# Block transposes for the second batch element's dense pairs, and up products between them

## The chip, the cores and the metric

The kernel runs on one core of a Trainium2 chip. The metric is the device time of one execution in microseconds (us); 1039.21 us is the median of three runs of the kernel before.

## What is computed

```python
q_assign = np.argmax(np.einsum('bhsd,hcd->bhsc', q_n, c_n), axis=-1)   # q, k, centroids normalised
k_assign = np.argmax(np.einsum('bhsd,hcd->bhsc', k_n, c_n), axis=-1)
mask = q_assign[:, :, :, None] == k_assign[:, :, None, :]
scores = scale * np.matmul(q, k.transpose(0, 1, 3, 2))
scores = np.where(mask, scores, -1000000000.0)
attn = np.exp(scores - scores.max(-1, keepdims=True))
attn = attn / (np.sum(attn, axis=-1, keepdims=True) + 1e-09)
x = np.matmul(attn, v)           # then (B,H,S,D) -> (B*S, H*D)
out = (x @ w_a) * (x @ w_b) @ w_out
```

The shapes are 4 batch elements, 8 heads, 768 tokens, head width 64, 16 clusters; model width 512, inner width 1536; all in fp32. The weights arrive as 64-bit numbers.

## The kernel before

Two heads make a pair, so there are 16 pairs, four to a batch element. Pairs 0 to 7 (batch elements 0 and 1) are computed densely: every score is formed and the mask is added as a product of one-hot cluster codes. The other eight are "sorted pairs" n = 1 to 8: their tokens are written to DRAM in the order of clusters, read back, and only scores within a cluster are formed. The feed-forward part follows for each batch element; its work is cut into pieces that a planner puts between other steps. All instructions are in an order that the program writes out while it is built, with a model clock (`now`, `clocks`, `spend`, `at`); on the chip each engine's queue runs in that order and waits on semaphores.

**Dense pairs** (`score`, `weigh`, `add_up`, `denominators`, `normalize`). A pair has two halves of 384 queries and six tiles of 128 keys, so 12 units; a group is two units, a pair six groups (l = 0 to 5), all of them 48. In each group TensorE forms the mask and the scores into two `ps_s` tiles (L497), ScalarE takes the exponential (L507), TensorE multiplies by v (L537), and the exponentials of a half are added up (L526), by GpSimd in pair 0 and by VectorE in the others, as two instructions of 128x384. Every third group the sums go through a product with ones (`denominators`, L555) and are inverted (L575 to L589).

**Preparing the next pair** (`prep_steps`). While pair p runs, pair p+1 is prepared step by step at l = 0 to 5: q and k are transposed on TensorE (`prep_transpose`, L361, copied out at L369), multiplied by the centroids (`prep_sim`, L377, L382), transposed back (`prep_across`, L388), turned into a one-hot on VectorE (`prep_assign`, L421 to L425, from `todo`), transposed as bf16 (`prep_onehot`, L434) and copied by ScalarE (L439, L442). `apart` gives these steps a tile: of `ps_m` as long as no feed-forward product has run, of `ps_s` afterwards.

**Sorted pairs** (`sorted_pair`). Each has a chain of steps with gaps and gates: `load_rows` (L1136), `across` (L1147, L1152), `similarities` (L1158), `assign` (L1178 to L1190), `prefix` (L1205, L1207), `index` (`find`, L1230 to L1257, and `after`), 24 indirect writes by GpSimd (`put`, L1308), `reload` (L1335, L1339), turns on VectorE (L1347), `scores` (L1376), `values` (L1401, L1410), `keep`, 12 indirect reads (`get`, L1440) and `x_across` (L1455). The first EARLY = 3 are sorted while the dense pairs run, in borrowed room; the rest after the dense pairs, in the tile `whole`, which takes their room (`late_room`). DRAM buffers go in a ring of three, cleared by `clear` (L1109, L1111).

**Weights** (`round_one`, `round_w`). Each of 36 parts is loaded (L278) and cut to fp32 by four VectorE instructions (L289 to L299), two of ScalarE (L303, L304) and an addition on GpSimd (L307).

**Feed-forward.** For batch element 0 the up products (`ffn_block`, pieces of 8 products over two column halves, L615) go block by block; the later batch elements and all down products use a scheme with seven products instead of eight (`ffn_ups`, `ffn_downs`). `in_turn` rotates three `ps_m` tiles. `PER_GROUP = 0` keeps all pieces out of the dense groups:

```python
    PER_GROUP = 0
    credit = 0
```

Each line of DMA on the sync engine (SP) is issued in order, and a waiting one holds the rest.

Of the kernel before, what the change touches and what calls it, by code (L numbers as in the profile page):

```python
# [34 lines left out]
P = 128  # L35
# [122 lines left out]
def short_path(nc, tc, ctx, c, cn, centroids_in, casts, n_far, q, k, v,  # L158
# [14 lines left out]
    SPACE, EARLY = 2.0, 3  # L173
# [4 lines left out]
    V, Vs, Vc, Vh, Vm, Vl = (Clocked(nc.vector, "V", us, *state)  # L178
                             for us in (0.56, 0.19, 0.29, 0.44, 0.7, 0.83))
    S_, Ss, Sl = (Clocked(nc.scalar, "S", us, *state) for us in (0.5, 0.3, 0.85))  # L180
    G_, Gi = (Clocked(nc.gpsimd, "G", us, *state) for us in (1.3, SPACE))
# [38 lines left out]

    def load(p):
        if p >= ND:
            return
        b, hp = divmod(p, HP)
        if p == 1:
# [26 lines left out]
    def load_v(p):  # L252
# [4 lines left out]
        vs[p] = t  # L257
        nc.sync.dma_start(
# [64 lines left out]

    idle = ps_o.tile([P, 512], FP32, name="O")
# [46 lines left out]
    def prep_sim(p):  # L371
# [4 lines left out]
        for kq in range(4):  # L376
# [3 lines left out]
                             start=True, stop=True)  # L380
        t = simp.tile([P, HB], FP32, name="sim")
# [78 lines left out]

    def prep_steps(p):
# [3 lines left out]
        def both(*fs):  # L465
            return lambda: [f() for f in fs]

# [50 lines left out]
    def add_up(u):  # L518
# [5 lines left out]
        acc = accs[p, hf]  # L524
        for a in range(2):
            (G_ if p == 0 else V).tensor_tensor(  # L526
                out=acc[:, a, :],
                in0=probs[u - 1][:, a, :] if j == 1 else acc[:, a, :],
                in1=probs[u][:, a, :], op=ALU.add)
# [89 lines left out]
    def store(b, j, half, y):  # L619
        rows = out[b * S:(b + 1) * S, :].rearrange(  # L620
            "(p j) (half n) -> p j half n", j=NJ, half=2)
# [21 lines left out]
    def ffn_block(b, blk):  # L643
# [14 lines left out]
        def piece_a(f):  # L658
# [3 lines left out]
            if f == 0:  # L662
# [3 lines left out]
                box["h"] = hp_.tile([P, NF, HB], FP32, name="h")  # L666
# [359 lines left out]
    kvd = [dram.tile([2 * ROWS + 32, 2 * D], FP32, name=f"kvd{n}") for n in range(3)]  # L1026
    qd = [dram.tile([2 * ROWS + 32, D], FP32, name=f"qd{n}") for n in range(3)]
# [14 lines left out]
    wanted = {}  # L1042
# [30 lines left out]
    def early_room():  # L1073
        t = hp_.tile([P, NF * HB], FP32, name="h")
        rooms([t[:, 0:ROW], t[:, ROW:2 * ROW]], extra[:, 2 * S:4 * S],
# [31 lines left out]
    def clear(n):  # L1107
        for m in range(n, NSORT, HP - 1):
            nc.sync.dma_start(out=od[m][2 * ROWS:], in_=zrow[0:32, 0:D])  # L1109
        for t, w in ((kvd[n % 3], 2 * D), (qd[n % 3], D)):  # L1110
# [11 lines left out]
    def sorted_pair(n, start):  # L1122
# [5 lines left out]
        parity, ring = n % 2, n % 3  # L1128
# [306 lines left out]
        def get(j, a):  # L1435
            if j == 0 and a == 0:
                if b not in xTs:
                    xTs[b] = xtp.tile([P, NCH, S], FP32, name="xT")
                M["xs"] = xTs[b][:, HP - 1].rearrange("p (j e) -> p j e", j=NJ)
# [40 lines left out]
        def may_load():  # L1480
            if n <= EARLY:
# [4 lines left out]
        chain += [plan(FREE, 7 if i == 0 else 0.3, lambda i=i: across(i),  # L1486
                       lambda: "P" not in busy and was("sims", n - 1), "T")
                  for i in range(3)]
# [6 lines left out]
                     lambda: was("clear", n, 8) if n < HP else was("reload", n - 3, 3))  # L1495
# [8 lines left out]
                     lambda: x_room() and (hp == 0 or was("x", n - 1)))  # L1504
# [518 lines left out]
```

## Time and profile before

| | |
|---|---|
| runs | 1038.17, 1039.21, 1040.02 us |
| profiled execution | 1039.23 us, its span 1037.2 us |
| TensorE (PE) busy | 985.5 us, 95% |
| VectorE (DVE) busy | 618.6 us, 60% |
| ScalarE (ACT) busy | 292.8 us, 28% |
| GpSimd (POOL) busy | 365.8 us, 35% |
| mean granted TensorE clock | 0.978 |

Busy times are shares of the span, from the first to the last instruction. "PEld" is TensorE's weight load, which overlaps its products. A row of the stretches gives the start and end, the length, and each engine's busy time in it with the number of instructions; then the granted clock, the DMA engines' share and GB/s. A row of a group gives line, engine, operation, tiles and shape, count, busy time, mean ns of one, and the idle time ahead of it with what ended it. A row of waits gives who waited for whom: us in total, times, longest.

### The profile page before, as it was taken

The page shows a single profiled execution, that of the slowest core. Times are in us where ns is not written, and L with a number is a line of the kernel's source. Part 1 is how long each engine was busy: PE and PEld are TensorE (multiplying, and loading weights), DVE is VectorE, ACT ScalarE, POOL GpSimd, SP SyncE. Part 2 cuts the span into 40 slices and gives each one's busy share as a digit, 9 for nine tenths or more (in the row PEclk, how much of TensorE's full clock was granted, in tenths as well). Part 3 has the DMA queues.
Part 4 walks back from the last instruction along what each step waited for, and adds up shares of the span by engine and source line. Part 5 has one row for each costly group of instructions (what it writes and reads, how often), then busy time and mean ns, then how long its engine had stood idle before and what let it go on. Part 6 is the DMA issues. An engine that isn't in the chain of part 4 may idle for free.

```text
span 1037.2 us, 20702 instructions
## 1 busy us (share of the span) xinstructions
PE 985.5 (95%) x8074; PEld 513.7 (50%) x8074; DVE 618.6 (60%) x1290; ACT 292.8 (28%) x609; POOL 365.8 (35%) x359
## 2 busy tenths in 40 slices
PE   8979998999799999989999899999999997999997
PEld 5434444443355545556444546654444763444564
DVE  5898897998476764846744775353335533334442
ACT  5636775775223322001122220021221101121100
POOL 3635563554105454433544453354441021000000
PEclk9989998999899999989999999999999998999999
DMA  9963642334978557392338533542327222222301
GB/s 235 248 155 103 169 144 63 94 102 110 184 151 168 152 120 121 122 179 59 88 76 145 119 83 131 106 113 79 82 75 155 87 52 60 59 62 61 118 29 32
DMA packets 242873, 116.51 MB, mean 112 GB/s; under 512 B 175696, under 2 KB 228944, under 8 KB 242768
## 3 DMA queue, kind: packets, MB, share of 16 engines
q1 hardware_dynamic: 233136, 102.08, 41.4%
q0 software_dynamic: 9216, 12.60, 4.8%
q8 instruction: 66, 1.08, 0.5%
q10 hardware_dynamic: 416, 0.43, 0.1%
q14 instruction: 39, 0.32, 0.1%
HBM read 79.46 MB, written 35.59 MB: 111 GB/s over the span
## 4 chain that ended last, share of the span: by engine, by line
PE 80%; DVE 12%; DMA 2%; SPq 2%; issue 2%; ACT 2%; POOL 0%; DVEq 0%; ACTq 0%
PE m L615 62%; PE s L497 4%; PE O L537 3%; DVE acc L526 3%; PE s L1376 2%; PE s L1401 2%; PE m L555 2%; PE s L1410 1%; SPq L1136 1%; PE m L361 1%; PE O L1147 1%; PE s L1455 1%; DVE rest L299 1%; DMA whole<-kvd 1%; SPq L1335 1%
## 5 line engine op out<-in xcount | busy, mean ns | idle before, releaser
L1440 POOL DMA_INDIRECT xT<-od,idx x96 | 94.3, 983 | 162.8 <-PE m L615 157.8
L615 PE MATMUL m<-xT,wb_sb 128*64 128x384 f32 x672 | 119.4, 494 | 1.3 <-DVE h L791 1.3
L615 PE MATMUL m<-xT,wa_sb 128*64 128x384 f32 x672 | 120.2, 495 | 0.0
L1308 POOL DMA_INDIRECT qd<-whole,idx x60 | 61.3, 1021 | 92.9 <-PE m L615 71.3
L791 DVE TENSOR_TENSOR ha<-ha,m 128x384 f32<-128x384 f32 x72 | 39.7, 551 | 89.6 <-PE m L615 68.6
L615 PE MATMUL m<-wo_sb,h 128*64 128x256 f32 x768 | 89.0, 387 | 0.0
L791 DVE TENSOR_TENSOR h<-h,m 128x384 f32<-128x384 f32 x72 | 39.8, 553 | 81.7 <-PE m L615 62.5
L788 ACT COPY h<-m 128x384 f32<-128x384 f32 x72 | 34.4, 478 | 187.4 <-PE m L615 184.1
L1308 POOL DMA_INDIRECT kvd<-whole,idx x60 | 61.3, 1022 | 66.7 <-PE m L615 57.3
L615 PE MATMUL m<-raw 128*64 128x384 f32 x432 | 79.0, 487 | 1.0 <-DVE raw L753 1.0
L507 ACT ACTIVATE pt<-s 128x768 f32<-128x768 f32 x96 | 72.7, 807 | 25.1 <-PE s L497 18.8
L615 PEld LDWEIGHTS m<-xT,wb_sb 128*64 128x64 f32 x672 | 48.2, 139 | 60.3 <-issue 53.8
L615 PEld LDWEIGHTS m<-xT,wa_sb 128*64 128x64 f32 x672 | 48.2, 139 | 58.5 <-issue 53.9
L537 PE MATMUL O<-pt,v 128*64 128x384 f32 x384 | 72.3, 498 | 0.0
L497 PE MATMUL s<-qkT 64*128 64x384 f32 x384 | 71.8, 494 | 0.0
L615 PEld LDWEIGHTS m<-wo_sb,h 128*64 128x64 f32 x768 | 55.5, 140 | 30.2 <-issue 3.7
L615 PE MATMUL m<-xT,h 128*64 128x256 f32 x576 | 65.0, 380 | 0.8 <-DVE h L903 0.8
L526 DVE TENSOR_TENSOR acc<-acc,pt 128x384 f32<-128x384 f32 x84 | 58.6, 754 | 2.4 <-ACT pt L507 2.4
L1308 POOL DMA_INDIRECT kvd<-h,idx x36 | 38.1, 1058 | 61.2 <-PE s L497 36.1
L615 PE MATMUL m<-xT,size 128*64 128x384 f32 x288 | 53.3, 491 | 3.0 <-DVE ha L791 3.0
L615 PEld LDWEIGHTS m<-xT,h 128*64 128x64 f32 x576 | 40.9, 137 | 21.8 <-issue 1.4
L615 PEld LDWEIGHTS m<-raw 128*64 128x64 f32 x432 | 30.6, 137 | 39.5 <-issue 36.8
(258 smaller groups left out, 1526.7 us busy)
## 6 DMA issues: line engine op xcount, KB each, us to landing
whole<-kvd SPq DMA_DIRECT2D x64, 160.0 KB
raw<-in_moe_w_a_dram SPq DMA_DIRECT2D x12, 512.0 KB
raw<-in_moe_w_b_dram SPq DMA_DIRECT2D x12, 512.0 KB
raw<-in_moe_w_out_dram SPq DMA_DIRECT2D x12, 512.0 KB
raw<-up_sums SPq DMA_DIRECT2D x96, 64.0 KB
whole<-qd SPq DMA_DIRECT2D x32, 160.0 KB
od<-whole SPq DMA_DIRECT2D x32, 160.0 KB
kvd<-xT SPq DMA_DIRECT2D x3, 1280.0 KB
```

The source lines that it names most:

```text
L497: ins = nc.tensor.matmul(out=s[:, a, 0:HB], lhsT=Ts[p][r, S + j * P:S + (j + 1) * P], rhs=Ts[p][r, hf * HB:(hf + 1) * HB], start=start, st ...
L507: Sl.activation(out=pt, in_=s[:, :, 0:HB], func=AF.Exp, scale=SCALE)
L526: (G_ if p == 0 else V).tensor_tensor(out=acc[:, a, :], in0=probs[u - 1][:, a, :] if j == 1 else acc[:, a, :], in1=probs[u][:, a, :], op=A ...
L537: ins = nc.tensor.matmul(out=O_of[0][a * D:(a + 1) * D, 0:HB], lhsT=vs[p][:, a, j, :], rhs=probs[u][:, a, :], start=(j == 0), stop=(j == N ...
L555: nc.tensor.matmul(out=ps[a * D:(a + 1) * D, 0:HB], lhsT=ones, rhs=t[:, a, :], start=(n == 0), stop=(n == len(terms) - 1))
L615: ins = nc.tensor.matmul(out=ps[half], lhsT=lhsT[:, half], rhs=rhs, **kw)
L788: S_.copy(out=box[name], in_=box["X"][:, 0:HB])
L791: V.tensor_tensor(out=box[name], in0=box[name], in1=box[bank][:, 0:HB], op=ALU.add)
L1308: ins = Gi.indirect_dma_start(out=dst[:, :], out_offset=bass.IndirectOffsetOnAxis(ap=M["idx"][:, w, j, a:a + 1], axis=0), in_=src, in_offs ...
L1376: nc.tensor.matmul(out=tiles[s // 2][r0:r0 + m, s % 2, c0:c0 + m], lhsT=M["skT"][r, h, 32 * x:32 * x + m], rhs=M["sqT"][r, h, 32 * x:32 * ...
L1401: nc.tensor.matmul(out=ps[:, s, 65 * i:65 * i + 65], lhsT=pt[:, P * i:P * i + P], rhs=vt[:, i, :], start=True, stop=True)
L1440: paced(Gi.indirect_dma_start(out=M["xs"][:, j, a * D:(a + 1) * D], out_offset=None, in_=od[n][:, :], in_offset=bass.IndirectOffsetOnAxis( ...
```

## The change

It does these things together:

- Pairs 4 to 7 (`by_blocks`) load q and k in 32-column blocks, so that VectorE's 32x32 block transposes give the transposed q and k, the transposed similarities, and the one-hot across; eight DMAs then place the one-hot's rows in `ohT`. TensorE's transposes and ScalarE's copies for these pairs go away. Their tokens keep the natural order, so v is loaded and the output is stored in it.
- The additions of pairs 1 to 7 become one instruction of 128x768.
- Feed-forward pieces are put into the dense groups: half a piece's cost is credited per group. Denominators then stand behind the next piece.
- Four sorted pairs are early instead of three (EARLY), and the DRAM ring has four buffers; their starts move to 76, 104, 150 and 150 of the model clock. The two `h` buffers are the borrowed room itself.
- Planner constants, gaps and gates change: the gap before a late pair's `across` is 12 instead of 7, before `x_across` 8 instead of 5; gathers may go ahead of the previous pairs' `x_across`.

```diff
-    SPACE, EARLY = 2.0, 3
+    SPACE, EARLY, RING = 2.0, 4, 4
...
+        if by_blocks(p):
+            t = qkp.tile([P, 2, S // 32, 32], FP32, name="qk")
+            for w, src in enumerate((q, k)):
+                for n in range(4):
+                    a, d = divmod(n, 2)
+                    nc.sync.dma_start(
+                        out=t[32 * n:32 * n + 32, w],
+                        in_=src[b, 2 * hp + a, :, 32 * d:32 * d + 32].rearrange(
+                            "(j t) d -> t j d", t=32))
...
+    def prep_by_blocks(p):
...
+        oh = oh_all[:, 0:3].rearrange("p n (g c) -> p (n g) c", c=NC)
+        ohT = oh_all[:, 3:6].rearrange("p n e -> p (n e)")
...
+        def across(w):
+            Vl.transpose(out=qkTs[p][:, w * S:(w + 1) * S],
+                        in_=qks[p][:, w].rearrange("p j d -> p (j d)"))
+
+        def sims_across():
+            V.transpose(out=sim.rearrange("p g c -> p (g c)"),
+                        in_=sims[p][:, 0:HB])
+
+        def one_hot():
+            V.tensor_tensor(out=oh[KT], in0=sim[KT], in1=top(first)[KT],
+                                    op=ALU.subtract)
+            V.tensor_tensor(out=oh[QT], in0=sim[QT], in1=top(first)[QT],
+                            op=ALU.is_equal)
+
+        def one_hot_across():
+            V.transpose(out=ohT, in_=oh.rearrange("p g c -> p (g c)"))
+            for a in range(2):
+                for kq in range(4):
+                    r = 32 * kq + a * NC
+                    nc.sync.dma_start(
+                        out=ohTs[p][a * D:a * D + NC, kq * HB:(kq + 1) * HB],
+                        in_=ohT[r:r + NC, :])
...
+        if p == HP:
+            return [[lambda: across(0), lambda: across(1)], [sims_across],
+                    assign[:2], assign[2:], [one_hot, one_hot_across], []]
+        return [[lambda: across(0), lambda: across(1)], [sims_across],
+                assign, [one_hot], [one_hot_across], []]
...
+        if p > 0:
+            Vd.tensor_tensor(out=acc, in0=probs[u - 1] if j == 1 else acc,
+                             in1=probs[u], op=ALU.add)
+            return
...
-                box["h"] = hp_.tile([P, NF, HB], FP32, name="h")
+                box["h"] = early[blk].rearrange("p (f t) -> p f t", f=NF)
...
-        chain += [plan(FREE, 7 if i == 0 else 0.3, lambda i=i: across(i),
+        chain += [plan(FREE, (12 if n > EARLY else 7) if i == 0 else 0.3, lambda i=i: across(i),
...
-                     lambda: x_room() and (hp == 0 or was("x", n - 1)))
+                     lambda: x_room() and (hp < 2 or was("x", n - (4 - hp))))
         chain += [plan(FREE, 0, lambda: mark("get", n)),
-                  plan(FREE, 5, x_across, kind="T")]
+                  plan(FREE, 8, x_across,
+                       lambda: hp == 0 or was("x", n - 1), "T")]
...
-                late = {"V": 2.2 if is_late else 7.0, "G": 1.8}.get(kind)
+                late = {"V": 2.2 if is_late else 4.0, "G": 2.6}.get(kind)
...
-            ffn.extend(counted(0, blocks[0][0][0:8]))
+            ffn.extend(counted(0, blocks[0][0]))
...
-            pieces = ups0[8:16] + ups[0:16] + ups0[16:24] + ups[16:24]
+            pieces = ups
...
-    PER_GROUP = 0
+    PER_GROUP = NCH * HB // 2
...
-    START, PERIOD = 14.0, 4.0
-    STARTS = [0.0, 36.0, 67.5, 99.0] + [190.0] * NPAIR
+    START, PERIOD = 16.0, 4.3
+    STARTS = [0.0, 76.0, 104.0, 150.0, 150.0] + [190.0] * NPAIR
...
-        at(t + (3.6 if i < 16 else 5.4), next_round)
+        at(t + 6.0, next_round)
...
-            if half[0] < ND:
+            if half[0] < ND and ffn:
+                ffn.insert(1, (0, lambda half=half: denominators(*half)))
+            elif half[0] < ND:
                 denominators(*half)
```

More of the change, by code (lines that the diff above doesn't have):

```diff
@@ L1633, in short_path @@
         sorted_pair(n, STARTS[n])
[L1634 to L1635 removed]
+    for n in range(1, RING + 1):
+        at((0.0, 16.0, 40.0, 64.0, 88.0)[n], lambda t, n=n: clear(n))
     for _ in range(12):
@@ L1668, in short_path @@
     early_room()
+    g = 0
     def tick(part):
-        now[0] += PERIOD * part
+        now[0] += (PERIOD if g < HP * GPP else 3.9) * part
         run_due()
     now[0] = START
-    for g in range(NG + 3):
+    for g in range(NG + 6):
         p, l = divmod(g, GPP)
```

92 lines of the change are left out of this document (69 added, 23 removed).

## The prediction

> **What bounds the kernel now.** I read the page's first two parts, then the stretches by stage, then what TensorE waited for, then the chain of waits, and last the single groups.
>
> ```profile
> span 1037.2 us, 20702 instructions
> ...
> PE 985.5 (95%) x8074; PEld 513.7 (50%) x8074; DVE 618.6 (60%) x1290; ACT 292.8 (28%) x609; POOL 365.8 (35%) x359
> ```
>
> TensorE (PE) is busy for 95% of the span, so only PE work taken away, or PE idle time filled, can count. VectorE (DVE) at 60% looks free. The stretches say where it is not. I cut them at the first mask product of each dense pair (pairs 0 to 7), then at the idle places behind them. Columns: length, then busy time of PE, weight load, DVE, ACT, POOL, then the granted clock.
>
> ```profile
> 14.10:41.90 27.80, 25.77 (x193) 12.86 (x192) 19.83 (x44) 18.36 (x33) 16.04 (x15) 1.00 1.02 230
> 41.90:80.20 38.30, 30.28 (x201) 14.05 (x201) 36.82 (x75) 18.92 (x36) 18.26 (x19) 0.87 0.70 181
> 80.20:106.50 26.30, 25.68 (x171) 11.78 (x171) 22.48 (x36) 17.57 (x35) 13.76 (x13) 1.00 0.38 103
> 106.50:133.60 27.10, 26.70 (x181) 12.60 (x181) 23.35 (x39) 19.65 (x40) 14.47 (x13) 1.00 0.70 176
> 133.60:169.00 35.40, 29.76 (x201) 13.96 (x202) 32.73 (x70) 19.86 (x40) 17.00 (x16) 0.90 0.31 89
> 169.00:194.80 25.80, 25.52 (x173) 11.75 (x172) 18.70 (x35) 16.86 (x32) 12.80 (x12) 1.00 0.36 98
> 194.80:220.80 26.00, 25.63 (x171) 11.72 (x170) 24.06 (x41) 19.58 (x40) 15.35 (x14) 1.00 0.34 106
> 220.80:245.00 24.20, 23.39 (x140) 9.78 (x140) 23.30 (x42) 17.55 (x37) 15.32 (x14) 1.00 0.35 105
> 245.00:280.00 35.00, 25.58 (x137) 10.57 (x134) 18.41 (x31) 9.18 (x22) 7.46 (x6) 0.90 0.86 166
> ...
> 440.00:480.00 40.00, 36.16 (x414) 23.18 (x410) 19.12 (x41) 4.70 (x9) 14.04 (x15) 0.91 0.63 127
> ...
> 555.00:580.00 25.00, 20.73 (x203) 9.76 (x203) 11.48 (x26) 4.62 (x9) 9.61 (x10) 0.93 1.10 186
> ...
> 855.00:880.00 25.00, 19.44 (x118) 8.98 (x114) 7.81 (x15) 3.19 (x6) 4.76 (x5) 0.86 0.23 62
> ```
>
> A quiet pair takes 26 to 27 us with DVE busy for 19 to 24 of them. Pairs 1 and 4, in which a sorted pair's list is made, take 38.3 and 35.4 with DVE full and a lowered clock. Behind the dense pairs four stretches leave PE idle. What ended those waits:
>
> ```profile
> PE m L555 <- DVE acc L526: 16.2, 6, 7.7
> PE O L1147 <- DMA whole<-in_q_dram: 11.1, 2, 7.2
> PE s L1455 <- DMA xT<-od,idx: 5.6, 2, 3.9
> PE m L615 <- DVE ha L791: 3.0, 1, 3.0
> ...
> PE m L615 <- DVE h L791: 1.3, 1, 1.3
> ```
>
> The 7.7 us is pair 1's. In order of time:
>
> ```profile
> 60.72 0.21 DVE L1230 TENSOR_REDUCE h<-h 128x32 f32<-128x64 f32 x1
> ...
> 68.68 1.02 DVE L526 TENSOR_TENSOR acc<-acc,pt 128x384 f32<-128x384 f32 x2
> 69.28 0.29 PEld L555 LDWEIGHTS m<-acc,ones 128*64 128x64 f32 x2 [8.38 <-DVE acc L526]
> ```
>
> From 60.72 DVE works through a sorted pair's places and the next dense pair's one-hot, 8.0 us, before the last addition for which the denominators (L555) wait. I call this the collision.
>
> **The change part by part.** In the order of the changed program the collision stands twice ahead of any feed-forward product, in pair 1 and now also in pair 2: additions, places, one-hot, addition, with the denominators behind. Pair 0 loses its sorted pair. The third chain stays in pair 4; a fourth (EARLY 4), which ran later, comes into pairs 5 and 6. Fourteen up products stand among the dense pairs, about one in two groups, 13 of them from pair 4 on; 11 more stand before the first late transposes, where five stood.
>
> Pairs 0 to 3. A chain on PE costs what pair 4 is busier than pair 5, 29.76 - 25.52 = 4.2, of which I count 3.5, since some of it is half clock: pair 0 -3.5. Pair 2 becomes a pair 1: 38.3 - 27.1 = +11 (bounds: +4 if only PE's part is felt, +12). Pair 1 stays. Pair 3 prepares pair 4 by the new way, so PE loses these:
>
> ```profile
> 172.20 1.29 PE m L555 x8
> 173.49 1.46 PE m L361 x12
> 174.95 1.72 PE s L497 x12
> 176.67 1.44 PE O L537 x8
> ...
> 277.27 2.73 PE m L615 x16
> ```
> ```profile
> L434 PE MATMUL m<-identb,h 128*128 128x128 bf16 x84 | 6.1, 220 | 0.0
> ```
>
> Twelve q and k transposes are 1.46, three of the similarities by the same price 0.4, twelve bf16 ones 12 x 6.1/84 = 0.9: -2.7. Against it, the one-hot now reaches PE by eight small DMAs instead of PE and ACT:
>
> ```profile
> 57.24 0.89 SPq L1109 DMA_DIRECT2D od<-xT  x2
> ```
> ```profile
> 456.60 4.12 DMA whole<-in_q_dram
> ```
>
> Eight issues at 0.89/2 = 3.6 us, and a landing between nothing and 4.1 us (a load of 192 KB, the nearest row, though far larger); I take 2, so 5.6 us behind DVE's transpose. Between that transpose's place and the next pair's scores stand a group (1.72 + 1.44) and an up product (2.73), 5.9 us. It is covered while DVE keeps up, and costs up to 4.1 - 0.3 where the landing is slow. In pair 3, +2.7 for it, net 0 (bounds -2.7 and +4). Pairs 0 to 3: -3.5 + 11 + 0 = **+7.5**, bounds 0 and +11.
>
> Pairs 4 to 7, PE. Six groups of 3.16 are 19.0, two denominators 2.6, similarities 0.5, so 22.1 a pair without chain or product, 88.4 for four; 13 products at 2.73 are 35.5; two chains 7: 131.
>
> The same, DVE. Before, 32.73 + 18.70 + 24.06 + 23.30 = 98.8. The additions in it:
>
> ```profile
> 133.60:245.00 111.40, 38.23 (x68) 0.00 (x0) 0.97 0.34 99
> ```
> ```profile
> L526 DVE TENSOR_TENSOR acc<-acc,pt 128x384 f32<-128x384 f32 x84 | 58.6, 754 | 2.4 <-ACT pt L507 2.4
> ```
> ```profile
> L1347 DVE STREAM_TRANSPOSE whole<-whole 128x640 f32<-128x640 f32 x32 | 25.9, 830 | 15.2 <-DMA whole<-kvd 7.6 <-DMA od<-whole 4.1 <-DMA whole<-qd 3.2
> ```
> ```profile
> 70.55 0.42 DVE L289 TENSOR_SCALAR wb_sb<-raw 128x512 int32<-128x512 int32 x1
> ...
> 72.19 0.69 DVE L299 SCALAR_TENSOR_TENSOR rest<-raw,rest 128x512 f32<-128x512 uint32 x1
> ```
>
> One addition of 768 replaces two of 384. It costs between 1.02 (the two that ran undisturbed at 68.68) and 2 x 0.754 = 1.5; 32 of them are 33 to 48, so -5 to +10, taken 0, nearer the undisturbed rate. Block transposes for three pairs: six of 768 at 0.830 x 768/640 = 1.0, six of 384 at half of that, and three more one-hot halves at 0.5: 10.5. One chain more is about what pair 4's DVE exceeds its neighbours', 32.7 - 22.0 = 11. One eviction of a product, and the last step of the 11 weight rounds that stood in this stretch:
>
> ```profile
> L673 DVE TENSOR_TENSOR h<-ha,m 128x384 f32<-128x384 f32 x24 | 13.2, 549 | 29.6 <-PE m L615 28.8 <-ACT size L304 0.7
> ```
> ```profile
> 133.60:245.00 111.40, 7.62 (x11) 0.97 0.34 99
> ```
>
> The six at 0.55 are 3. The order shows three or four more rounds from pair 4 on, at 72.88 - 70.55 = 2.3: 8. Sum 98.8 + 10.5 + 11 + 3 + 8 = 131, bounds 126 and 141.
>
> Both engines stand at 131, and PE's waits do not coincide with DVE's, so I take 140 (bounds 131, everything hidden, and 152, DVE's high bound and 11 of waits: one collision). The same work took 111.4 + 35.5 + 3.5 = 150.4: **-10**, bounds -19 and +2.
>
> A rule speaks against this part: the Trainium skill (VectorE: DVE Perf Modes, Rules for kernel authors) keeps 128x128 transposes on TensorE wherever the result may go to PSUM. By it the sum would lose its -10, and end near 1025. No row here has DVE in TensorE's place, so the trace does not settle it.
>
> In this stage similarities, denominators and the sorted transposes also leave the three ps_m tiles for the two ps_s tiles of the scores, so a score waits for DVE or ACT to read them. The product behind each covers 2.73; uncovered they cost part of the 9 us by which 140 exceeds 131.
>
> SP's queue gets 32 one-hot DMAs, 16 q/k loads more (32 of 128-byte rows where 16 of 256-byte rows stood), four v loads more, and the fourth chain's eight row loads and one clear. POOL gets that chain's 24 indirect writes earlier:
>
> ```profile
> L1308 POOL DMA_INDIRECT qd<-h,idx x36 | 38.1, 1059 | 23.5 <-PE s L497 8.7 <-PE O L537 7.5 <-issue 4.5
> ```
> ```profile
> q1 hardware_dynamic: 233136, 102.08, 41.4%
> ```
>
> 24 x 1.06 = 25 us on a POOL that was busy for 60 of these 111: free. Packets: 0.414 x 16 x 1037.2 / 233136 = 29 ns each, so a pair's 6144 take 6144 x 29 ns/16 = 11 us, of a whole pair's time ahead: hidden; if the cover were gone, the 11 us would stand at the start of a pair.
>
> Behind the dense pairs. The first late transposes waited 7.2 us for q and the second 3.9; six more products (16.4 us) stand before the first, and the planned gap is 12 instead of 7, which covers both: -11.1. The gathers' 5.6: the last gather is planned 3 us earlier against the transposes and may start before the pair before has ended: -5.6. The 3.0 + 1.3 at 565 to 575 fall in a burst (DMA share 1.10) in which a late pair's loads are issued between the sums' stores; in the new order no such load stands there, but a reload just ahead does: -1. Lowered clock in these stretches: 35 x 0.10 + 40 x 0.09 + 25 x 0.07 + 25 x 0.14 = 12.3, mostly inside the waits; I take back 4.3. Together **-22**, bounds -5 (the gathers alone) and -28.
>
> Sum: 1037.2 + 7.5 - 10 - 22 = 1012.7 of span. The profiled execution took 1039.23, so 2.0 lie around the span, and the median of the runs, 1039.21, is the same: **1015 us**.
>
> **The rivals.**
> First, DVE keeps what the products give. For it: DVE full in pairs 1 and 4, and two collisions ahead of the products. Against it: the products' 35.5 us are time in which DVE can catch up. Both stages at their upper bound: 1037.2 + 11 + 2 - 22 + 2 = 1030 (1024 to 1036). The rule of the Trainium skill on transposes (above) is this case.
>
> Second, the one-hot DMAs are late, and the kernel slower. SP issues in order, and what stands ahead of them are weight loads:
>
> ```profile
> SPq L278 <- DVE rest L299: 99.4, 19, 10.3
> ```
>
> Such a load holds SP for 5.2 us in the mean, 10.3 at most, until DVE has rounded. If that happens at the four pair boundaries, PE idles there 5.2, and 2.5 of half clock follow (in pair 1 the stretch of 38.3 at clock 0.87 lost 5.0, half of it inside its wait): 4 x 7.7 = 31, so 1046. It decides from 26/4 = 6 us a boundary. Against it: in the new order the rounds that free these buffers stand ahead of the transpose on DVE itself.
>
> Third, deeper: the collisions shrink because pairs 1 and 2 have shorter additions, the second stage hides everything: 1037.2 + 0 - 19 - 26 + 2 = 994.
>
> Fourth, the late waits only move to other places and the dense stages cancel: 1037.2 + 7.5 - 10 + 3 + 2 = 1040, no change. That the products are not interleaved at all is excluded by the order.
>
> **How the numbers follow.** Forecast 0.60, its own range 1001 to 1026; first rival 0.17; second 0.13; third 0.06; fourth 0.04. About 0.2%, 2 us, is what a measurement of this kernel can tell from no change. Faster: 0.60 + 0.17 + 0.06 = 0.83; same 0.04; slower 0.13. The range takes the first rival in, and most of the third: 997 to 1037 leaves out the second, the fourth and the third's deep half, 0.20.
>
> **What would show it.** Right: pairs 1 and 2 both near 38 us with the denominators waiting for the addition; pairs 4 to 7 in about 140 us with 13 up products; no wait for q or for the gathers beyond 2 us; the wide addition near 1.0 us. Wrong: mask products waiting for the one-hot's DMAs over 3 us a pair; the stage from pair 4 above 150; a new wait of the same size behind the dense pairs.

## The result, and the profile after

The changed kernel takes 1068.89 us (median of four runs, 1068.31 to 1069.22) where the kernel before takes 1038.84 beside it: ratio 1.0287, 95% interval 1.0270 to 1.0305. The change is slower by 30 us; 1015 was forecast. From the page of the kernel after, span and busy times:

```profile
span 1067.2 us, 20492 instructions
...
PE 984.4 (92%) x7966; PEld 526.2 (49%) x7966; DVE 608.9 (57%) x1256; ACT 280.3 (26%) x586; POOL 367.6 (34%) x359
```

TensorE's busy time is what it was (985.5 before), though the trace has 108 of its instructions fewer; the 30 us are idle TensorE. The stretches, cut as before: the eight dense pairs, then five places behind them (length, busy PE, PEld, DVE, ACT, POOL, granted clock):

```profile
14.10:42.40 28.30, 24.24 (x160) 11.54 (x161) 15.32 (x31) 16.51 (x29) 20.12 (x19) 0.95 0.82 192
42.40:81.40 39.00, 32.52 (x211) 15.58 (x210) 28.29 (x54) 19.88 (x39) 5.67 (x4) 0.86 0.81 210
81.40:117.10 35.70, 29.17 (x195) 13.29 (x195) 27.59 (x53) 18.51 (x36) 13.61 (x13) 0.90 0.52 123
117.10:148.60 31.50, 25.78 (x160) 10.37 (x159) 25.72 (x37) 16.80 (x35) 22.41 (x20) 1.00 0.50 121
148.60:190.00 41.40, 37.43 (x227) 16.57 (x227) 33.42 (x54) 21.54 (x43) 25.09 (x22) 0.92 0.64 141
190.00:231.30 41.30, 36.98 (x223) 15.98 (x224) 32.40 (x63) 18.16 (x35) 20.18 (x20) 0.92 0.56 131
231.30:268.50 37.20, 31.74 (x201) 13.27 (x199) 30.07 (x58) 15.63 (x31) 17.85 (x17) 1.00 0.22 62
268.50:297.30 28.80, 27.46 (x174) 11.96 (x174) 26.24 (x38) 17.67 (x35) 22.85 (x19) 1.00 0.39 115
330.00:355.00 25.00, 20.74 (x234) 9.93 (x232) 16.33 (x30) 8.33 (x16) 4.77 (x4) 0.86 0.53 145
480.00:515.00 35.00, 31.38 (x332) 17.02 (x328) 22.08 (x54) 5.77 (x10) 13.10 (x14) 0.90 0.53 118
620.00:660.00 40.00, 27.59 (x228) 17.39 (x228) 16.55 (x35) 2.98 (x7) 10.01 (x10) 0.83 0.77 166
700.00:730.00 30.00, 23.84 (x242) 12.04 (x240) 12.61 (x23) 5.07 (x9) 10.68 (x12) 0.89 0.70 142
760.00:785.00 25.00, 17.46 (x158) 8.44 (x154) 10.49 (x19) 2.87 (x6) 8.15 (x9) 0.86 0.67 114
```

The dense pairs end at 297.3, where they ended at 245.0 before. By then 12.25 of the 14 products have run (196 instructions, 16 to a product). The same work before (245.0, 12.25 x 2.73 = 33.4, one chain more at the forecast's 3.5) would come to 281.9: +15.4, where -2.5 was forecast. Behind them it is 769.9 against 1037.2 - 281.9 = 755.3: +14.6, where -22 was forecast. So both stages missed, and the larger miss lies behind the dense pairs. What ended TensorE's waits in the kernel after (us in all, times, longest):

```profile
PE m L644 <- DVE acc L611: 14.1, 3, 6.5
PE m L704 <- DMA comb<-up_sums: 13.5, 2, 7.5
PE m L704 <- DMA raw<-down_sums: 12.4, 1, 12.4
PE O L1238 <- ACT whole L1243: 4.3, 1, 4.3
PE s L582 <- DMA ohT<-h: 4.0, 3, 2.0
PE s L582 <- ACT acc L649: 3.9, 8, 0.9
...
PE m L1238 <- DMA h<-in_q_dram: 3.4, 1, 3.4
PE m L704 <- DVE rest L1016: 3.3, 1, 3.3
```

The late pairs' waits for q (11.1) and for the gathers (5.6) are gone; the 3.4 us for q is an early chain's, at 40.47. In their place TensorE waits 25.9 us for loads of kept sums (up_sums, down_sums), which it did not wait for before, and the clock is lowered behind each of these waits: 40 x 0.17 + 30 x 0.11 + 25 x 0.14 = 13.6 us of granted clock lost in the last three stretches, in part inside the waits. The longest of them in order of time, SP's issues and then TensorE:

```profile
617.54 1.27 SPq L979 DMA_DIRECT2D xT<-down_sums  x3
618.91 0.56 SPq L1227 DMA_DIRECT2D whole<-in_q_dram  x1
...
624.70 1.89 SPq L1227 DMA_DIRECT2D whole<-in_v_dram  x1
626.64 3.20 SPq L1426 DMA_DIRECT2D whole<-qd  x4
629.93 4.64 SPq L1426 DMA_DIRECT2D whole<-kvd  x4
634.62 3.33 SPq L1430 DMA_DIRECT2D whole<-kvd  x4
637.99 2.69 SPq L979 DMA_DIRECT2D raw<-down_sums  x4
```
```profile
627.68 2.11 PE L704 MATMUL m<-xT,h 128*64 128x256 f32 x18
642.21 3.25 PE L704 MATMUL m<-raw,ha 128*64 128x256 f32 x14 [12.41 <-DMA raw<-down_sums]
```

Between the third and the fourth load of down sums SP issues the 8 row loads of one sorted pair and the 12 reloads of another: 618.91 to 637.95, 19 us. TensorE uses up what it has and stands. At 703 and 756 twelve reloads stand in the same way between loads of up sums, and TensorE waits 6.0 and 7.5 us. In the kernel before, reloads stood between stores and outputs, or, once (787.85 to 798.29), ahead of down sums that TensorE came to only at 802.64.

### The profile page after: what moved, and what is told of

It reads as the page before. It is cut to its first block, busy times and chain, and to the rows that moved or that the text cites. A ratio compares the mean times of both kernels' runs of the same rounds, so it can differ in the third digit from the quotient of the medians.

```text
span 1067.2 us, 20492 instructions
## 1 busy us (share of the span) xinstructions
PE 984.4 (92%) x7966; PEld 526.2 (49%) x7966; DVE 608.9 (57%) x1256; ACT 280.3 (26%) x586; POOL 367.6 (34%) x359
## 4 chain that ended last, share of the span: by engine, by line
PE 43%; issue 6%; POOL 3%; SPq 2%; DMA 1%; DVE 1%; POOLq 0%; ACT 0%; DVEq 0%
PE m L704 40%; POOL kvd L1399 2%; POOL qd L1399 2%; PE s L1467 1%; SPq L1430 1%; SPq L1426 1%; PE s L1492 1%; PE s L1501 1%; DMA comb<-up_sums 1%; PE s L1547 1%; DVE raw L809 0%; DMA od<-whole 0%; SPq L840 0%; DVE whole L1438 0%; DVE xT L809 0%
## 5 line engine op out<-in xcount | busy, mean ns | idle before, releaser
L704 PE MATMUL m<-xT,wb_sb 128*64 128x384 f32 x672 | 116.1, 487 | 0.0
L881 DVE TENSOR_TENSOR ha<-ha,m 128x384 f32<-128x384 f32 x72 | 39.8, 552 | 101.0 <-PE m L704 81.3
L881 DVE TENSOR_TENSOR h<-h,m 128x384 f32<-128x384 f32 x72 | 39.8, 553 | 84.5 <-PE m L704 61.5
L1399 POOL DMA_INDIRECT qd<-whole,idx x48 | 47.2, 983 | 95.0 <-PE m L704 91.5
L582 PE MATMUL s<-qkT 64*128 64x384 f32 x384 | 75.8, 512 | 0.0
L626 PE MATMUL O<-pt,v 128*64 128x384 f32 x384 | 74.7, 511 | 0.0
L1399 POOL DMA_INDIRECT kvd<-whole,idx x48 | 48.9, 1018 | 64.2 <-PE m L704 49.2
L1399 POOL DMA_INDIRECT kvd<-h,idx x48 | 50.1, 1043 | 38.6 <-PE O L626 14.2
L1399 POOL DMA_INDIRECT qd<-h,idx x48 | 53.2, 1109 | 28.8 <-PE s L582 11.7
L878 ACT COPY ha<-m 128x384 f32<-128x384 f32 x54 | 25.8, 478 | 102.6 <-PE m L704 102.6
```

The costliest lines, as they stand in the source:

```text
L582: ins = nc.tensor.matmul(out=s[:, a, 0:HB], lhsT=Ts[p][r, S + j * P:S + (j + 1) * P], rhs=Ts[p][r, hf * HB:(hf + 1) * HB], start=start, st ...
L626: ins = nc.tensor.matmul(out=O_of[0][a * D:(a + 1) * D, 0:HB], lhsT=vs[p][:, a, j, :], rhs=probs[u][:, a, :], start=(j == 0), stop=(j == N ...
L704: ins = nc.tensor.matmul(out=ps[half], lhsT=lhsT[:, half], rhs=rhs, **kw)
L878: S_.copy(out=box[name], in_=box["X"][:, 0:HB])
L881: V.tensor_tensor(out=box[name], in0=box[name], in1=box[bank][:, 0:HB], op=ALU.add)
L1399: ins = Gi.indirect_dma_start(out=dst[:, :], out_offset=bass.IndirectOffsetOnAxis(ap=M["idx"][:, w, j, a:a + 1], axis=0), in_=src, in_offs ...
```

## Experiments

The chips of these runs took 1044 to 1046 us for the kernel before, so ratios to it are compared, each with its 95% interval. "Dense end" is the start of the weight load of pair 7's last score products in the trace (after 293.9; before 241.9, or 274.7 with 12 products at 2.73). In every run with products among the dense pairs, 12 of the 14 stand ahead of it.

| run | ratio | dense end |
|---|---|---|
| after | 1.0287 (1.0270 to 1.0305) | 293.9 |
| e1_sums_by_act | 1.0197 (1.0144 to 1.0251) | 290.1 |
| e2_gaps_back | 1.0333 (1.0287 to 1.0379) | 294.3 |
| e3_no_blocks | 1.0266 (1.0207 to 1.0325) | 300.5 |
| e5_no_mix | 1.0165 (1.0125 to 1.0206) | 264.4 |
| f1_starts_back | 1.0251 (1.0188 to 1.0315) | 273.7 |
| f2_starts_back_no_mix | 1.0276 (1.0236 to 1.0315) | 258.1 |
| e4_before_gaps | 1.0232 (1.0179 to 1.0285) | 241.4 |
| h2_sums_by_act_turns_later | 1.0050 (1.0032 to 1.0068) | 293.7 |
| h3_turns_only | 1.0114 (1.0061 to 1.0167) | 293.6 |
| m1_starts_act_turns | 0.9915 (0.9891 to 0.9938) | 285.3 |
| m2_before_act_turns | 1.0170 (1.0145 to 1.0194) | 240.9 |
| m3_three_early_act_turns | 1.0103 (1.0074 to 1.0132) | 273.7 |
| m4_wide_act_turns | 1.0104 (1.0060 to 1.0149) | 242.9 |
| e7_before_wide | 1.0142 (1.0102 to 1.0182) | 242.3 |
| n1_m1_no_blocks | 1.0044 (1.0024 to 1.0064) | 299.3 |
| n2_m1_no_mix | 1.0114 (1.0052 to 1.0176) | 259.0 |
| n3_m1_sums_by_sp | 0.9999 (0.9976 to 1.0022) | 285.1 |
| n4_m1_gaps_back | 0.9982 (0.9964 to 0.9999) | 283.6 |

### The kept sums on another queue

```diff
-                        nc.sync.dma_start(out=dst[c], in_=kept[:, c])
+                        nc.scalar.dma_start(out=dst[c], in_=kept[:, c])
...
-                    nc.sync.dma_start(out=B[name][i], in_=kept(i))
+                    nc.scalar.dma_start(out=B[name][i], in_=kept(i))
```

> The loads of the kept up and down sums (L840, L979) are issued by ScalarE's queue instead of SP's; nothing else differs from the kernel after (1068.9 us). Theory, SP's order: behind the dense pairs the kernel after loses 12.4 + 6.0 + 7.5 = 25.9 us to three waits for kept sums whose loads stand in SP's queue behind 8 row loads and 12 reloads, and 10 to 14 us of half clock follow them. Then these waits fall to under 2 us each and the time to 1030 to 1043; the dense stage still ends near 297. Rival 1, the sums themselves or their transfers are late whichever queue issues them: the waits stay, 1062 to 1072. Rival 2, ScalarE's queue holds the loads up behind its own waits: the three waits go, but new waits for up_sums or down_sums of 10 us or more in all stand elsewhere, 1045 to 1060.

The ratio fell to 1.0197, about a third of what the waits and their clock had seemed worth, and none of the three expected cases came. The waits for sums fell from 25.9 us to 1.9, and others of half the size took their place. From TensorE's waits of this run, then VectorE in order of time, then SP's longest wait between 690 and 715 us:

```profile
PE m L704 <- DVE ha L881: 13.0, 2, 6.8
```
```profile
711.29 1.57 DVE L1438 STREAM_TRANSPOSE whole<-whole 128x640 f32<-128x640 f32 x2 [5.15 <-DMA whole<-kvd]
...
713.39 0.56 DVE L881 TENSOR_TENSOR ha<-ha,m 128x384 f32<-128x384 f32 x1
```
```profile
SPq L1426 <- DMA raw<-up_sums: 6.1, 1, 6.1
```

VectorE's turns of the sorted pair wait for the reload, and the feed-forward's addition (L881), for which TensorE waits, stands behind them in VectorE's queue. A late reload now blocks through another in-order queue. What makes it late is new: in the kernel after, SP issued the twelve reloads from 703.39 on with no wait between them; here it stops three times among them, for 6.1, 4.1 and 3.7 us, until loads of up sums have landed that ScalarE's queue issued. Why SP waits for these is not shown. The next runs plan the turns later, together with the sums' queue and alone:

```diff
-        chain += row(FREE, 6, turns + masking, "V", lambda: was("keep", n - 1, 4))
+        chain += row(FREE, 18, turns + masking, "V", lambda: was("keep", n - 1, 4))
```

> The sums' loads by ScalarE's queue, as in the run at 1.0197, and the planned gap from a reload to VectorE's turns of it 18 instead of 6. There the waits for sums had gone, but two waits of 6.8 and 6.2 us for an addition (L881) stood in their place, behind turns (L1438) on VectorE that waited for the reload. Theory, it is the reload's lateness that passes down whichever in-order queue stands behind it: with the turns planned later these two go as well, -10 to -16, ratio 1.003 to 1.012. Rival, they are TensorE's loss to something else at these places (clock, transfers): ratio 1.015 to 1.025. A risk: the late pairs end later, and the last feed-forward waits for the gathers, 1.02 and over.

> The kernel after with turns 18 instead of 6 after the reload, the sums' loads left on SP's queue. In the built order the nine down loads now stand together ahead of the row loads, while two reloads still stand among the up loads. Theory of SP's order: the wait for down_sums (12.4) goes, two waits for up_sums of 4 to 8 us stay, each with 3 to 7 of half clock: ratio 1.012 to 1.022, between after (1.0287) and the same with the loads on ScalarE's queue (1.0050). Rival, the turns alone made that gain: 1.003 to 1.009.

Both edits give 1.0050: 0.2 us of waits for sums are left, and for `h` of L881 1.3 us. The turns alone give 1.0114, just below the expected range, with two waits for sums left where the order has reloads between up loads. The later turns also change the built order: the nine down loads stand together in it, as expected. From TensorE's waits of the turns alone:

```profile
PE m L704 <- DMA raw<-up_sums: 5.3, 1, 5.3
...
PE m L704 <- DMA comb<-up_sums: 3.2, 1, 3.2
```

So about 25 us of the 30 lost (1.0287 to 1.0050) go when the sums leave SP's queue and the turns stand further behind a reload; each edit alone gave 9 and 18.

### The longer gaps

In the kernel after both gaps go back; in the kernel before they are put in alone.

```diff
-        chain += [plan(FREE, (12 if n > EARLY else 7) if i == 0 else 0.3, lambda i=i: across(i),
+        chain += [plan(FREE, 7 if i == 0 else 0.3, lambda i=i: across(i),
...
-                  plan(FREE, 8, x_across,
+                  plan(FREE, 5, x_across,
```

> The planner's gaps ahead of a late pair's across and x_across go back from 12 and 8 to 7 and 5; the rest is the kernel after. In the built order the row loads and the reload still stand between the loads of kept sums: 3 loads, 8 row loads, 3 loads, 12 reloads, 3 loads, and twice 12 reloads among the up sums. Theory, SP's order: the waits for kept sums stay at 20 to 30 us in all, and 5 to 11 us of waits for q (L1238) come back: 1065 to 1080. Rival, the gaps are what moved the reloads into the way: waits for sums under 10 us, 1040 to 1055.

> The kernel before, with only the two planned gaps of the change (12 instead of 7 before a late pair's across, 8 instead of 5 before x_across). The prediction's term for the stage behind the dense pairs, tried alone: the waits for q (11.1) and the gathers (5.6) go, -12 to -22, ratio 0.979 to 0.989. Theory of SP's order: the built order now has a reload among the up loads and one among the down loads of a later batch element, where before had them among stores or outputs, so 8 to 18 us of waits for sums come in: ratio 0.995 to 1.005.

The first came out as the theory said: 20.1 us of waits for sums (11.4, 6.2, 2.5) and 8.8 for q, ratio 1.0333. The second was worse than either expectation: these two numbers alone make the kernel before 2.3% slower. Waits for sums are only part of it. From TensorE's waits there, then SP and TensorE in order of time:

```profile
PE O L1147 <- ACT whole L1152: 11.0, 2, 8.0
PE m L615 <- ACT rest L936: 10.1, 1, 10.1
```
```profile
464.18 2.01 SPq L1335 DMA_DIRECT2D whole<-qd  x4
...
480.73 1.01 SPq L1136 DMA_DIRECT2D whole<-in_v_dram  x1
481.84 0.74 SPq L641 DMA_DIRECT2D out_dram<-comb  x1
```
```profile
470.73 5.35 PE L615 MATMUL m<-xT,h 128*64 128x256 f32 x48
486.19 4.10 PE L615 MATMUL m<-raw,ha 128*64 128x256 f32 x20 [10.11 <-ACT rest L936]
```

Here the blocked instruction is an output's store at 481.84, behind 12 reloads and 8 row loads (464.18 to 481.74). Its buffer is needed by ScalarE's next copy, and the copy by TensorE. So the mechanism is not tied to the sums: whatever the built order puts behind such a burst of 20 DMAs on SP is issued later by what the burst takes, 17.6 us here (1.3 of it a wait for TensorE) and 19 in the kernel after.

### The starts, the fourth early chain and the products, in the changed kernel

Starts back, three early chains (`f1`); the same without products among the dense pairs (`f2`); after without products (`e5`); after without blocks (`e3`):

```diff
-    SPACE, EARLY, RING = 2.0, 4, 4
+    SPACE, EARLY, RING = 2.0, 3, 4
...
-                     lambda: now[0] > 64 and was("clear", n, 8) if n <= RING
+                     lambda: was("clear", n, 8) if n <= RING
...
-    STARTS = [0.0, 76.0, 104.0, 150.0, 150.0] + [190.0] * NPAIR
+    STARTS = [0.0, 36.0, 67.5, 99.0] + [190.0] * NPAIR
```
```diff
-    PER_GROUP = NCH * HB // 2
+    PER_GROUP = 0
...
-            if half[0] < ND and ffn:
-                ffn.insert(1, (0, lambda half=half: denominators(*half)))
-            elif half[0] < ND:
+            if half[0] < ND:
```
```diff
     def by_blocks(p):
-        return HP <= p < ND
+        return False
```

> The kernel after, but with three early sorted pairs at the starts of before (0, 36, 67.5, 99 of the model clock, indirect writes not held until 64); products, blocks, wide addition, ring of four and gaps stay. Pair 0 took 27.8 us with a chain before and 28.2 without one after, so a chain there is free, while each chain after cost its pair 4 to 11. Theory, the moved and added chains lengthen the dense stage: pairs 0 to 7 end 10 to 16 us earlier than after (297.3, so 281 to 287), of which a fifth late pair takes some 7 back; with late waits for sums as after the ratio to before is 1.012 to 1.023 (after 1.0287). Rival, the products and the shared score tiles lengthen the dense stage: its end moves by under 5 us and the ratio stays at 1.025 to 1.035.

> As the run with three early pairs at their old starts, and also no up product among the dense pairs. Leaving the products out alone brought the ratio from 1.0287 to 1.0165. If products and starts act apart, the two gains add: ratio 0.998 to 1.012, and the dense pairs end at 245 to 252. If the products only hurt because the chains crowd the same pairs, the gain is that of the starts alone: 1.012 to 1.020. The nine down loads of one half stand together with nothing between, two reloads stand among the up loads, so waits for up_sums of 8 to 15 us remain.

> No up product is put among the dense pairs (denominators stand where they stood before); block transposes, wide addition, starts and gaps stay as after. 14 products of 2.73 = 38.2 us leave the dense stage, which ended at 297.3 after. If they covered nothing, it ends at 259; by the prediction's terms VectorE (122 us measured in pairs 4 to 7, 131 forecast) then bounds pairs 4 to 7, which take 115 to 125 instead of 148.7 - 35.5 = 113, so the end lies at 262 to 271. In SP's order the nine down loads stand together now, and the reloads stay among the up loads: theory of SP's order, the wait for down_sums (12.4) goes and 10 to 15 us of waits for up_sums stay, in all 1055 to 1070. Rival, the order on SP does not matter: waits for sums of 25 us as after, and 1070 to 1085.

> All eight pairs are prepared by TensorE transposes; the products among the dense pairs, the wide addition, the starts and the gaps stay as after. Pairs 4 to 7 took 148.7 us after. By the prediction's terms TensorE gets back 2.7 us a pair for three or four pairs, +8 to +11, and VectorE loses 10.5: if TensorE bounds the stage, 156 to 160; if what bounds it is VectorE or the way over ohT's DMAs and two shared score tiles, 138 to 147. SP's order has 6 loads of sums, 8 row loads, 3 loads, 12 reloads, and 12 reloads twice among the up sums, so by the theory of SP's order waits for sums of 12 to 25 us stay behind the dense pairs: 1050 to 1075 in all. Rival, blocks cause the late waits too: below 1045.

With three early chains the dense end comes 20 us earlier, more than expected, and the time hardly moves: behind the dense pairs 20.7 us of waits for sums and 14.1 for the last gathers stand. Without products the dense end is 29.5 earlier where the 12 ahead of it took 32.8, so they cover 3.3; without them TensorE waits longer for the one-hot's DMAs (4.0 us in the kernel after):

```profile
PE s L582 <- DMA ohT<-h: 16.6, 7, 6.7
```

Yet the time falls: the nine down loads now stand together, and the wait of 12.4 is gone. Both edits together give no more than one, outside both expectations; 9.4 us of waits for up sums, 12.3 for the copies of L1243 and 9.1 for those of L1026 stand there. Without blocks pairs 4 to 7, from the first mask product of pair 4 to the dense end, take 8.5 us more than in the kernel after, as expected. Read by their times alone, these runs would say that the blocks do nothing, the products cost 12 us and the starts nothing; the late stage hides all three.

### A version with the late waits taken away

`m1`: the two edits of `h2`, four early chains, and the first three at the starts of before, their indirect writes not held until 64 of the model clock.

```diff
-    STARTS = [0.0, 76.0, 104.0, 150.0, 150.0] + [190.0] * NPAIR
+    STARTS = [0.0, 36.0, 67.5, 99.0, 150.0] + [190.0] * NPAIR
```

> The run at 1.0050 (sums' loads by ScalarE's queue, turns 18 after the reload), with the first three chains at the starts of before (36, 67.5, 99; the fourth at 150) and their indirect writes not held until 64. A chain in pair 0 was free there, and pairs 0 to 3 took 134.4 us. With three early pairs at these starts the pairs 0 to 3 took 131.6 in another run, with a chain in each of pairs 0, 1 and 3. Theory, the place of the chains costs in the dense stage: its end comes 4 to 10 us earlier than 297, and the ratio falls to 0.995 to 1.002. Rival, what is won there is lost to the collision of two chains in pairs 3 and 4: 1.002 to 1.010.

> The kernel before, with the two edits that brought the changed kernel from 1.0287 to 1.0050: the sums' loads by ScalarE's queue, and turns 18 instead of 6 after the reload. The kernel before has no wait for sums, so nothing of that kind is to be won. Theory, SP's order and no more: the waits for q (11.1) shrink by up to 8 because SP is free of some 200 loads, the later turns delay the last gathers by 5 to 10: ratio 0.990 to 1.008. Rival, ScalarE's queue or the later turns are better in themselves by what they gave there: 0.975 to 0.985.

> The version at 0.9915 with three early sorted pairs instead of four. With three (and the sums on SP) the dense pairs ended at 277, with four at 288.7, so the fourth costs 11.7 there. Theory, it pays that back behind the dense pairs, where a fifth late pair costs its list, its turns on the queues and a last gather that TensorE waits for (13 to 18 us of such waits in the runs with five late pairs): ratio 0.995 to 1.012. Rival, the fourth early chain is a loss: 0.978 to 0.988.

`m1` is faster than both kernels, 0.9915, and better than expected. The longest of TensorE's waits are its collisions, in pairs 1 and 3 (at 69 and 128 us):

```profile
PE m L644 <- DVE acc L611: 11.3, 2, 6.8
```

The same two late edits make the kernel before slower (`m2`, 1.0170, more than expected), and three early chains instead of four (`m3`) bring 1.0103, although the dense end is 11.6 earlier. In both, five pairs are sorted late, and the last gathers are not there in time (14.5 us of waits in `m2`). That the later turns do this is shown only in the kernel before (5.6 there): `f1` waits 14.1 with the turns at 6, and `f2`, also with five late pairs, not at all. TensorE's wait for the gathers in `m3`:

```profile
PE s L1547 <- DMA xT<-od,idx: 14.2, 6, 3.9
```

So the edits are no gain in themselves, and the fourth early chain, 11.6 us in the dense stage, pays for itself behind it.

### The wide addition alone

The kernel before with additions of 128x768 in pairs 1 to 7 (`e7`), and the same with the two late edits (`m4`):

```diff
+        if p > 0:
+            Vl.tensor_tensor(out=acc, in0=probs[u - 1] if j == 1 else acc,
+                             in1=probs[u], op=ALU.add)
+            return
         for a in range(2):
```

> The kernel before, with additions of 128x768 in pairs 1 to 7 and nothing else. In the trace after, one took 0.996 to 1.095 us where two of 384 took 1.51 before: 42 of them save VectorE 17 to 21 us. Where VectorE is full (pairs 1 and 4) TensorE may win 2 to 6 us; so by itself the edit gives -2 to -8 us in the dense stage, 0.992 to 0.998. Theory of SP's order: the model clock shifts by it, and the built order has a reload among the up loads, one between the down loads, where before had them elsewhere: +6 to +18 of waits for sums or for what stands behind the reloads, so ratio 1.000 to 1.015.

> The kernel before with the wide additions, the sums' loads by ScalarE's queue, and turns 18 after the reload. Theory: the dense stage gains what the wide addition alone gains (0 to 8 us), and the waits that its shifted order would bring behind the dense pairs cannot stand: ratio 0.982 to 0.998. Rival, the later turns delay the last pairs' gathers and the last batch element waits for them: 1.000 to 1.010.

The dense end does not move (242.3 and 242.9, before 241.9), so the addition gains nothing by itself there: in `e7` TensorE waits 20.9 us for additions, 16.2 before. The shifted order behind it costs 1.4%. With the two late edits 1.0% of loss remains, as the rival said, with 14.4 us of waits for the gathers.

### The forecast's own terms, tried in the faster version

Each takes one part out of `m1`: the blocks, the products, the sums' queue, the gaps; the edits are those shown above.

> The version at 0.9915 without block transposes (TensorE transposes for all pairs). Behind the dense pairs SP's order is the same, so the dense stage's difference should come through undiminished. In the changed kernel the blocks cost pair 3 some 3 us and saved pairs 4 to 7 8.2 (156.8 without, 148.6 with). Theory, that difference of 5 to 10 us is what they are worth: ratio 0.996 to 1.001. Rival, it is absorbed behind them: 0.988 to 0.995.

> The version at 0.9915 with no up product among the dense pairs. In the changed kernel, taking them out left the dense stage 267 us long where 38.2 us less than 297.3 would have been 259: the products cover some 8 us of waits there. With no waits for sums possible behind the dense pairs, that shows in the time: ratio 0.996 to 1.003. Rival, what the run without them in the changed kernel seemed to say (1.0165 against 1.0287), the products cost 12 us: 0.978 to 0.985.

> The version at 0.9915 with the loads of the kept sums back on SP's queue. In the built order 12 reloads stand ahead of six down loads and 12 more between 8 and 32 up loads. Theory of SP's order: two waits for sums of 5 to 12 us each come back, with 3 to 7 us of half clock behind each, ratio 1.003 to 1.017. Rival, the starts and the later turns alone made the gain: 0.989 to 0.996.

> The version at 0.9915 with the two late gaps back at 7 and 5. The prediction gave the longer gaps 11.1 (q) and part of 5.6 (gathers). Theory, they are worth what they cover, the waits for q of the late pairs come back with 5 to 11 us: ratio 0.996 to 1.002. Rival, their worth is nothing, since an across that is placed later comes no earlier in SP's queue: 0.988 to 0.994.

Without blocks the dense end is 14.0 later and the ratio 0.0129 higher, 13.5 us, more than expected: what the blocks win in the dense stage arrives at the end. The rule cited in the prediction (the Trainium skill, VectorE: DVE Perf Modes, Rules for kernel authors) speaks of 128x128 transposes; here the loads place the blocks so that transposes of 32x32 do. The loss that the prediction drew from it for this part did not come.

Without products the ratio is 0.0199 higher, 21 us, more than expected. In the dense stage they covered 259.0 - (285.3 - 32.8) = 6.5. The rest lies behind it: the products that then come at once meet weights that are not cut yet (10.2 us), and 8.8 us are a blocked queue again. From that run's waits of TensorE, then VectorE in order of time:

```profile
PE m L704 <- POOL wa_sb L327: 10.2, 2, 5.3
PE m L704 <- DVE raw L843: 8.8, 1, 8.8
```
```profile
513.55 0.49 DVE L843 TENSOR_TENSOR comb<-wa_sb 128x128 f32<-128x128 f32 x2 [10.09 <-DMA out_dram<-comb]
```

VectorE's sum of weights needs a buffer whose output SP stores only at 510.93, behind twelve reloads and four other stores that it issues from 495.05 on. So 21 us is not the products' worth alone.

With the sums back on SP two waits return, smaller than expected (rows of `n3`), and the gain is gone: 0.9999. With the gaps back the q wait returns (row of `n4`), 0.9982, as expected.

```profile
PE m L704 <- DMA xT<-down_sums: 3.9, 1, 3.9
...
PE m L704 <- DMA comb<-up_sums: 3.3, 1, 3.3
```
```profile
PE O L1238 <- DMA whole<-in_q_dram: 5.4, 1, 5.4
```

The Trainium skill (DMA: Bandwidth & Descriptors, Issuing engines are not separate DMA queues) holds that issuing from several engines saves only the sequencer's time, "usually small relative to the DMA itself". For one DMA the traces agree: about 0.9 us of issue in a burst, beside the 4.12 us of a load of q in the prediction's row. In a burst of 20 that time is the cost: 17.6 and 19 us of SP's issuing ahead of one transfer, and 0.0084 of the time, 9 us, between `n3` and `m1`.

## Why the prediction was wrong

**The step that failed** is "Behind the dense pairs. ... Together -22", with bounds -5 to -28, both of them gains. The waits it named did go: q by 11.1, the gathers by 5.6. What it left out is that the change moves the late pairs' row loads and reloads against the loads of kept sums, on a queue that issues both in order. The text noted that "a reload just ahead does" stand in the new order, and let it take 3.3 of a gain of 4.3; for a load of sums behind a reload it has no term. Its own sign of being wrong, "a new wait of the same size behind the dense pairs", is what came. Measured: -11.1 and -5.6, the 4.3 of before gone, 4.3 for L1243's copy, 25.9 for sums, 3.3 for L1016, which is +12.5; and the clock, 12.3 lost before, 13.6 + 25 x 0.14 + 35 x 0.10 = 20.6 after, +8.3. That is +20.8, in part counted twice, against the stage's +14.6. `h2` gets 25 of the change's 30 us back, `n3` loses 9 again with the sums on SP, and `e4` shows the same kind of wait in the kernel before. Which part of the change moved the loads is not shown: with the gaps back (`e2`) or three early chains (`f1`) waits of this kind stay, and the gaps alone (`e4`) or the wide addition alone (`e7`) bring some to the kernel before.

The fourth rival, "the late waits only move to other places", names what happened there, with a chance of 0.04; but it expected no change, and its price (+3) was taken from the waits that left, where three waits for sums came to 25.9. The second rival named SP's queue too, but another place: the waits for the one-hot's DMAs are 4.0 us in all, not 31. They are short with the products there; in `e5`, without them, they are 16.6.

**Pairs 0 to 3**, +7.5 with bounds 0 and +11. Measured 134.5 with one product, 131.8 without it, against 119.5 before: +12.3. Pair 2 did become a pair 1, 35.70 against 26.30: +9.4. (The prediction subtracted 27.10, which is pair 3's row; its term should have been +12, not +11.) Pair 0's chain was not worth 3.5: without it the pair takes 28.30 where it took 27.80 with it, so it had been free. `m1`, with a chain there again, has its dense end 8.4 earlier than `h2`. Pair 3, forecast at net 0, took 4.4 more, 2.7 of it the product. (The price of a slow landing there, 4.1 - 0.3, counts the 2 us twice that the 5.6 already holds: 3.6 + 4.1 - 5.9 = 1.8.)

**Pairs 4 to 7**, 140 us in bounds 131 to 152, measured 148.7, with 133.6 of TensorE busy, 131 forecast. These sums took 13 products; by the stage's end 11.25 have run (180 instructions), so 1.75 x 2.73 = 4.8 comes off each: 126 for TensorE, 135 for the stage with an upper bound of 147, and 145.6 for the same work before. By that the stage is 3 slower where -10 was forecast.

```profile
148.60:297.30 148.70, 133.62 (x818) 57.79 (x820) 122.13 (x211) 72.99 (x144) 85.96 (x77) 0.95 0.46 113
```
```profile
145.80:277.00 131.20, 122.47 (x748) 52.50 (x750) 113.04 (x173) 70.01 (x139) 57.29 (x45) 0.97 0.37 96
```

The first row is the kernel after, the second `f1`, whose three chains have all their TensorE work ahead of pair 4; both have as many products there. Without the two chains it is 17.5 us less. The term that was too small is the chain's: 3.5 on TensorE each, where two cost 11.1 of its busy time and 6.4 us beside it. The wide addition's length was right (row below; 1.0 forecast), VectorE's sum 122 against 131.

```profile
L611 DVE TENSOR_TENSOR acc<-acc,pt 128x768 f32<-128x768 f32 x42 | 41.8, 996 | 2.1 <-ACT pt L592 0.7
```

Without chains the gain forecast for this stage is mostly there: 131.2 in `f1` against 111.4 + 11.25 x 2.73 - 3.5 = 138.6 for the same work before. In `m1` the blocks alone are worth 13.5 at the end. In this change it did not reach the end: the four chains stood in worse places than in `m1`, and the late stage was out of step. The slower pace of the weight rounds, the ring of four and the gate of the gathers were not tried alone.

## What to carry to other kernels

When an edit moves steps that issue DMAs, write down, for the new order, what stands behind every burst on that queue and when it is needed; a wait that goes is only a gain if the queue's next urgent transfer is not late instead. A stage that was tuned around one in-order queue can make an upstream edit look bad: measure an edit's worth in a version in which the late waits cannot stand, by another queue or more distance. Two numbers in a plan (12 for 7, 8 for 5) cost 2.3% in one order and gained 0.7% in another, so they cannot be judged by the wait that they cover.

## What was not expected of the hardware

Issuing 20 plain DMAs took SP 19.0 us in one place and 17.6 in another (1.3 of it a wait), some 0.9 us each, with one issue of a reload in the kernel after between 0.3 and 2.8 us; what sets this length was not tried. A row that merges several issues can also hold waits: in `e1` four issues of a reload stand in one row of 7.90 us at 693.59, and 6.1 of it are the wait for up sums shown above, while no issue took more than 0.53.

Open: what ties SP's issues to the loads of ScalarE's queue in `e1`, why `m1` came out some 4 us better than expected, and whether its collisions in pairs 1 and 3, 11.3 us of its waits, can be taken away; none of these was tried.
